# Agent attention and a gated feed-forward layer on one core: value runs in other gaps, query splits a gap earlier, both matmuls of a weights call together, the output copy ahead of a subtraction

## The chip, the cores and the metric

The kernel runs on one core of a Trainium2 chip. The metric is the device time of one execution in microseconds (us), lower is better. TensorE (PE) multiplies, VectorE (DVE) and ScalarE (ACT) do the element-wise work, GpSimd (POOL) issues some copies as DMAs, and SyncE (SP) issues the loads and the stores.

## The reference, cut to what matters

```python
def _attn_ref(q, k, v, agents):          # q, k, v: 4 x 12480 x 128, agents: 4 x 49 x 128
    scale = 1.0 / np.sqrt(q.shape[-1])
    def sm(a, b):
        s = scale * (a @ b.transpose(0, 2, 1))
        s = s - s.max(-1, keepdims=True)
        e = np.exp(s)
        return e / (e.sum(-1, keepdims=True) + 1e-09)
    agent_v = sm(agents, k) @ v           # 49 x 128 per batch
    return sm(q, agents) @ agent_v

def _moe_ref(x, w_in, w_out):            # x: 49920 x 128, w_in: 128 x 2048, w_out: 2048 x 128
    h = x @ w_in
    g = h * (1.0 / (1.0 + np.exp(-1.702 * h)))
    return g @ w_out                      # x is the attention's output
```

All is float32. For each of the 4 batches the agents attend to the keys and gather the values, then every query attends to the 49 agents, and the result goes through the feed-forward layer.

## The kernel before, in words

The attention's last product is folded into the first feed-forward weight: for each batch `agent_v @ w_in` is computed once (49 x 2048, `weights_parts`), and a token then needs only its 49 softmax weights. Float32 products are made from two or three parts of lower precision (`hi` and `lo`, `wh` and `wl`, `gh` and `gl`), so each large product is three matmuls. The matmuls work on half of PE's rows, two at a time, one on each half (`half_matmul`).

Queries are handled in blocks of 960 tokens: 13 blocks per batch, 52 in all (`n`). A block has 16 feed-forward steps `f` of 128 columns. One step is an `up` (6 half matmuls into two banks of the pool `ph`, which has four), two GELUs on ACT (L493) that free those banks, a rounded copy `gh` (a POOL-issued DMA, or ACT, L505), a remainder `gl = g - gh` on DVE (`low`, L510), and a `down` (12 half matmuls into the output banks `po`).

The program is a list of gaps. A block has 17 of them (k = 0 to 16). In a gap each engine gets, in this order: the extra jobs that a table put there (`put`), the `up` of a step, the `low` of the step three before, the `down`s of a step about five before (one half of two steps), and the `high`s. Gap k = 1 has no `up`. At k = 16 (`NF`) the only down is the last half of the block's last step, and `store` copies the two `po` banks out, one by ACT (L540) and one by DVE (L542). The next block's first `down`, in its gap 0, writes the same two banks. Each engine runs its own instructions in exactly this order; only SP's order is left to the framework.

The extra jobs for the blocks to come are:

- Query block n + 1: its tile is split on DVE in four pieces (L170, L172; tile `rest`) in gaps 13 to 16, scored on PE in gaps 0 and 1 of the next block, shifted by its maximum in gap 2, exponentiated on ACT in gap 4 (with a change of ACT's function table before and after), summed and scaled in gap 6, transposed in gap 8 (`P_AT`).
- Keys of the next batch, three groups in a block at gaps 4, 10 and 13 (`K_AT`), 13 groups, so the first four to five blocks of a batch: the key phase.
- Then the values of the next batch, the value phase of seven blocks: two key groups are exponentiated together on ACT in gap 4 (`E_AT`, L320, `slot`), each group's pair of operands `e_pair` (high part and remainder, DVE L325 and L326) is made in gap 7, the pair `v_pair` from a value tile (DVE L330 and L331) in gaps 6 and 10, and the value runs (`key_values`, 16 half matmuls of 258 columns) are in gaps 10 and 14 (`V_AT`). `key_sum` adds the result in the gap behind (L353).
- Then the weights of the next batch: `weights_1` and two calls of `weights_parts` of 1024 columns each, two banks in a call. Six such calls are at the three batch boundaries, one more near the program's start.

The extra jobs' results on PE (scores, transposes, value runs, weights) all go through one two-bank tile, `ps_m`, of a pool with a single buffer.

Of the kernel before, what the change touches and what calls it, by code (L numbers as in the profile page):

```python
# [18 lines left out]
TB = 120  # L19
# [10 lines left out]
Z_AT = 6  # L30
P_AT = 8
K_AT = (4, 10, 13)
V_AT = (6, 10)
PAIR = 2 * 128 + 16
BY_DMA = (1, 9)
EPS = 1e-09
# [3 lines left out]
def kernel(  # L40
# [10 lines left out]
    nc = tc.nc  # L51
    B, C, N = qT.shape
    A = agT.shape[2]
    F = w_in.shape[1] // 2
    NF = F // P
# [25 lines left out]
    for c in range(2):  # L81
        nc.vector.tensor_add(
            out=sel[:, c * H : c * H + A], in0=ident[:, 0:A], in1=ident[:, H : H + A]
# [3 lines left out]
    for i in range(2):  # L87
        t = const.tile([P, KB, P], F32R, name=f"e_pair{i}")
        nc.gpsimd.memset(t.bitcast(F32), 0.0)
        e_pair.append(t)  # L90
    v_pair = const.tile([P, KB, 2 * C + 2], F32R, name="v_pair")
# [71 lines left out]
    def split(t):  # L163
        r = work.tile([P, GT + PAD], F32, name="rest", tag="rest")
        nc.gpsimd.memset(t[:, GT:], 0.0)

        def piece(i):
            s = slice(0, CH + PAD) if i < 2 else slice(CH + PAD, GT + PAD)
            if i % 2 == 0:
                nc.vector.tensor_sub(out=r[:, s], in0=t[:, s], in1=halves(t)[0][:, s])  # L170
            else:
                nc.vector.tensor_sub(out=halves(r)[1][:, s], in0=r[:, s], in1=halves(r)[0][:, s])  # L172

        return (halves(t)[0], halves(r)[0], halves(r)[1]), piece
# [30 lines left out]
    def two_banks():  # L205
        return ps_m.tile([P, 2, 512], F32, name="ps_m")
# [115 lines left out]
    def key_pair(g):  # L322
        sc = score[:TB, g * KB : (g + 1) * KB, :]
        ep = e_pair[g % 2]
        nc.vector.tensor_copy(out=ep[:TB, :, 0:A], in_=sc)  # L325
        nc.vector.tensor_sub(out=ep[:TB, :, H : H + A], in0=sc, in1=ep[:TB, :, 0:A].bitcast(F32))  # L326

    def value_pair(vt):
        vp = v_pair
        nc.vector.tensor_copy(out=vp[:TB, :, 0:C], in_=vt[:TB])  # L330
        nc.vector.tensor_sub(out=vp[:TB, :, C : 2 * C], in0=vt[:TB], in1=vp[:TB, :, 0:C].bitcast(F32))  # L331

    def key_values(g):
# [57 lines left out]
    def weights_parts(b, w, c, banks=(0, 1)):  # L391
        if c == 0 and 0 in banks:
            wts[b] = wpool.tile([P, F], F32R, name="wh"), wpool.tile([P, F], F32R, name="wl")
        wh, wl = wts[b]
        pw = two_banks()
        for i in banks:
            s = slice((c + i) * 512, (c + i + 1) * 512)
            nc.tensor.matmul(out=pw[:, i], lhsT=w["avT"], rhs=w_in_sb[:, s], start=True, stop=True)  # L398
            nc.scalar.copy(out=wh[:, s], in_=pw[:, i])
            nc.vector.tensor_sub(out=wl[:, s], in0=pw[:, i], in1=wh[:, s].bitcast(F32))  # L400

# [146 lines left out]
    vts = {}  # L548
# [5 lines left out]
    banks = {}  # L554
# [14 lines left out]
    def do_query_load(n):  # L569
        if n < B * NG:  # L570
            qts[n] = query_load(*divmod(n, NG))
# [6 lines left out]
    def do_query_split(n, i):  # L578
        if n < B * NG:
            if i == 0:  # L580
                q_parts[n], pieces[n] = split(qts.pop(n))
            pieces[n](i)
# [6 lines left out]
    def do_key_store(b, g):  # L589
        key_store(g, banks.pop((b, g))[1])  # L590
# [9 lines left out]
    def do_query_scores(n, c):  # L600
        if n < B * NG:
            if c == 0:
                banks[n] = score_banks()
            scores(n // NG, q_parts[n], banks[n][0], c)

    def do_query_shift(n):
        if n < B * NG:
            scored[n] = query_shift(banks.pop(n)[1])

    def do_query_exp(n):  # L610
        if n < B * NG:
            query_exp(scored[n])

    def do_query_sums(n):
        if n < B * NG:
            sums[n] = query_sums(n)

    def do_query_softmax(n):
        if n < B * NG:
            query_softmax(n, scored.pop(n), sums.pop(n))  # L620

    def do_query_pairs(n):
        if n < B * NG:
            pairs[n] = query_pairs(n)
# [102 lines left out]
    def gap_of(u):  # L727
        if u < LAG:
            return u
        n, k = divmod(u - LAG, NF)  # L730
        return LAG + n * GAPS + (k + 1 if k else 0)

    def put(t, fn):
        at.setdefault(t, []).append(fn)

    def take(t, runs):
        assert not busy.intersection(range(t, t + runs)), t
        busy.update(range(t, t + runs + 1))
# [8 lines left out]
    for n in range(B * NG):  # L747
        t = LAG + n * GAPS
        m = n + 1
        for i in range(4):  # L750
            put(t - 4 + i, lambda m=m, i=i: do_query_split(m, i))
        take(t, 2)
        put(t, lambda m=m: do_query_scores(m, 0))
        put(t + 1, lambda m=m: do_query_scores(m, 1))
        put(t + 2, lambda m=m: do_query_shift(m))
        put(t + 2, lambda m=m: do_query_load(m + 1))
        put(t + E_AT, lambda m=m: do_query_exp(m))
        put(t + Z_AT, lambda m=m: do_query_sums(m))
        put(t + Z_AT, lambda m=m: do_query_softmax(m))
        take(t + P_AT, 1)  # L760
        put(t + P_AT, lambda m=m: do_query_pairs(m))
# [9 lines left out]
    for b in range(B - 1):  # L771
        begin = gap_of(b * NG * NF)
        end = gap_of((b + 1) * NG * NF)
        slots = [LAG + n * GAPS + k for n in range(B * NG) for k in K_AT]
        slots = [t for t in slots if t >= begin + 4][:NKG]
        for k, t in enumerate(slots):
            put(max(t - 13, 0), lambda b=b, k=k: do_key_load(b + 1, k))
            for i in range(4):
                put(t - 4 + i, lambda b=b, k=k, i=i: do_key_split(b + 1, k, i))
            take(t, 2)  # L780
            put(t, lambda b=b, k=k: do_key_scores(b + 1, k, 0))
            put(t + 1, lambda b=b, k=k: do_key_scores(b + 1, k, 1))
            put(t + 2, lambda b=b, k=k: do_key_store(b + 1, k))
        mx = {}
        put(t + 3, lambda mx=mx: key_max_0(mx))
        t = free(t + 4)
        put(t, lambda mx=mx: key_max_1(mx))
        t = free(t + 2)
        put(t, lambda mx=mx: key_max_2(mx))
        shift = t + 1  # L790

        n0 = (shift + 1 - LAG - E_AT + GAPS - 1) // GAPS
        for k in range(NKG):
            slot = LAG + (n0 + k // 2) * GAPS + E_AT
            exps.setdefault(slot, []).append(k)
            last = k == NKG - 1
            t = slot + V_AT[k % 2]
            put(min(shift + 3 * k, slot - 1), lambda k=k: key_shift(k, nc.vector.tensor_tensor))
            put(t - 16, lambda b=b, k=k: do_value_load(b + 1, k))
            put(t - 4, lambda b=b, k=k: value_pair(vts.pop((b + 1, k))))  # L800
            put(slot + 3, lambda k=k: key_pair(k))
            take(t, 1)
            put(t, lambda b=b, k=k: do_key_values(b + 1, k))
            put(t + 1, lambda b=b, k=k: do_key_sum(b + 1, k))
        w = {}
        put(t + 2, lambda b=b, w=w: weights_0(accs.pop(b + 1), w))
        t = free(t + 3)
        put(t, lambda w=w: weights_1(w))
        for c in range(0, F // 512, 2):
            t = free(t + 2)  # L810
            assert t < end + 4 * c - 3, (b, begin, shift, end, t)
            put(t, lambda b=b, w=w, c=c: weights_parts(b + 1, w, c))
# [23 lines left out]
    def do_low(u):  # L836
        if 0 <= u < steps:
            gl[u] = low(g.pop(u), gh[u])
# [11 lines left out]
    def gap(t):  # L850
        n, k = divmod(t - LAG, GAPS)
        final = n == B * NG - 1
        if t < LAG:
            u = t
        elif final:
            u = n * NF + LAG + k
        elif k == 1:
            u = None
        else:
            u = n * NF + LAG + max(k - 1, 0)  # L860
        before, late[:] = list(late), []
        rest()
        for job in at.pop(t, ()):
            job()
        if u is not None:
            if u < steps:
                do_up(u)
                rest()
            do_low(u - 3)
        if t >= LAG:  # L870
            do_downs(n, k)
        for u in before + soon:
            do_high(u)
        soon.clear()

    def do_downs(n, k):
        if k == 0:
            po[n] = [ps_o.tile([P, 512], F32, name=f"po{c}") for c in range(2)]
        first_whole = NF - LAG - 1 if n == B * NG - 1 else NF
        if 0 < k <= first_whole:  # L880
            do_down(n, k - 1, True)
        if k < first_whole:
            do_down(n, k, False)
        elif k < NF:
            do_down_whole(n, k)
        else:
            store(*divmod(n, NG), po.pop(n))
# [44 lines left out]
```

## Time and profile before

| | |
|---|---|
| time, median of 3 runs | 1999.68 us (1998.36 to 2003.41) |
| profiled execution, its time | 2000.02 us |
| its span, first to last instruction | 1998.2 us |
| PE busy | 1939.2 us, 97% |
| PE weight loads (PEld) busy | 1800.3 us, 90% |
| DVE busy | 1557.0 us, 78% |
| ACT busy | 1397.0 us, 70% |
| mean granted PE clock | 0.988 of full speed |

The span is 1.8 us shorter than the time, so differences in the span are differences in the time. PE is the engine with the most work. PE's busy time is drawn from modelled ends of pipelined matmuls, so a stretch that looks filled need not run at PE's own pace; the distance between the starts of the same matmul in successive gaps tells more.

### The profile page before, as it was taken

To read this page: it belongs to the slowest core of one execution; us is meant where nothing else is said; L and a number is where in the kernel's file an instruction comes from. 1 tells how busy PE (TensorE), PEld (TensorE's weight loads), DVE (VectorE), ACT (ScalarE), POOL (GpSimd) and SP (SyncE) were. 2 spreads that over 40 slices of the span, in tenths; PEclk is the share of its full clock that TensorE was granted. 3 is DMA by queue.
4 is the path that set the end of the run, shared out by engine and by line. 5 is a ranking of instruction groups with operands and counts; after the bars stand their busy time and mean duration, and the time that the engine had idled before them with its cause. 6 is when DMAs were issued, how large, how long until landed. Compare 5 with 4: busy or idle time off the path is not lost.

```text
span 1998.2 us, 59378 instructions
## 1 busy us (share of the span) xinstructions
PE 1939.2 (97%) x25150; PEld 1800.3 (90%) x25150; DVE 1557.0 (78%) x2037; ACT 1397.0 (70%) x2406; POOL 291.0 (15%) x639
## 2 busy tenths in 40 slices
PE   7699999999999999999999999999999999999999
PEld 7489999999889999998988999999997999999998
DVE  6588878888778888887877888888876767676775
ACT  3257777677667667777667667777676777777775
POOL 0011111111111111111111111111111111111111
PEclk9699999999999999999999999999999999999999
DMA  9466566665545565665655566566654554545453
GB/s 279 137 187 205 181 190 187 197 193 189 179 159 191 184 199 180 189 199 181 195 163 170 190 200 192 186 198 190 189 169 141 173 182 169 189 169 189 169 178 140
DMA packets 118383, 366.96 MB, mean 184 GB/s; under 512 B 12604, under 2 KB 32284, under 8 KB 118116
## 3 DMA queue, kind: packets, MB, share of 16 engines
q0 software_dynamic: 75168, 256.61, 37.3%
q1 hardware_dynamic: 42948, 106.55, 19.6%
q8 instruction: 197, 3.23, 0.7%
q14 instruction: 70, 0.57, 0.1%
HBM read 80.97 MB, written 25.56 MB: 53 GB/s over the span
## 4 chain that ended last, share of the span: by engine, by line
PE 85%; ACT 5%; DVE 5%; DMA 4%; issue 2%; SPq 0%; DVEq 0%; POOLq 0%; POOL 0%; ACTq 0%
PE po L191 47%; PE ph L191 26%; PE ps_m L191 8%; DMA gh<-g 2%; ACT g L493 1%; DVE gl L510 1%; ACT L493 1%; PE ph L260 1%; ACT L419 1%; PE ps_m L398 1%; DMA words<-w_out 1%; ACT score L320 1%; DMA vt<-v 1%; DVE rest L172 0%; PE po L532 0%
## 5 line engine op out<-in xcount | busy, mean ns | idle before, releaser
L493 ACT ACTIVATE g<-ph 128x480 f32<-128x480 f32 x1664 | 851.8, 571 | 454.0 <-PE ph L191 445.2
L510 DVE TENSOR_TENSOR gl<-g,gh 128x960 fp32r<-128x960 f32 x832 | 945.8, 1153 | 230.7 <-DMA gh<-g 138.5
L191 PE MATMUL po<-gh,wo_h 64*128 64x480 f32 x3300 | 833.9, 381 | 5.8 <-DVE o L542 3.9
L191 PE MATMUL po<-gl,wo_h 64*128 64x480 f32 x3300 | 826.8, 378 | 0.0
L191 PE MATMUL po<-gh,wo_l 64*128 64x480 f32 x3300 | 822.3, 376 | 0.0
L503 POOL DMA_DIRECT2D gh<-g x522 | 275.7, 528 | 1647.7 <-PE ph L191 722.7
L191 PEld LDWEIGHTS po<-gh,wo_h 64*128 64x128 f32 x3300 | 488.5, 184 | 24.1 <-DVE o L542 10.7
L191 PEld LDWEIGHTS po<-gh,wo_l 64*128 64x128 f32 x3300 | 490.0, 184 | 13.2
L191 PEld LDWEIGHTS po<-gl,wo_h 64*128 64x128 f32 x3300 | 491.5, 186 | 11.3
L191 PE MATMUL ph<-q_hi,wh 49*128 49x480 f32 x1664 | 443.8, 404 | 10.1 <-ACT g L493 9.4
L191 PE MATMUL ph<-q_lo,wh 49*128 49x480 f32 x1664 | 420.2, 381 | 0.0
L191 PE MATMUL ph<-q_hi,wl 49*128 49x480 f32 x1664 | 415.9, 378 | 0.0
L505 ACT CAST gh<-g 128x960 fp32r<-128x960 f32 x310 | 310.5, 1002 | 8.2
L191 PEld LDWEIGHTS ph<-q_hi,wh 49*128 49x128 f32 x1664 | 247.5, 185 | 42.8 <-ACT g L493 28.4
L191 PEld LDWEIGHTS ph<-q_hi,wl 49*128 49x128 f32 x1664 | 247.6, 185 | 9.3 <-DVE wl L400 0.2
L191 PEld LDWEIGHTS ph<-q_lo,wh 49*128 49x128 f32 x1664 | 247.5, 188 | 4.3
L191 PE MATMUL ps_m<-ag_part,rest 64*128 64x49 bf16 x4320 | 146.6, 182 | 7.6 <-DVE rest L172 4.9
L191 PEld LDWEIGHTS <-rest 64*128 64x128 bf16 x4320 | 126.2, 93 | 9.8 <-DVE rest L172 7.1
L172 DVE TENSOR_TENSOR rest<-rest 128x488 bf16<-128x488 f32 (+1 forms) x182 | 131.8, 724 | 0.1
L191 PE MATMUL ps_m<-ag_part,qt 64*128 64x49 bf16 x2448 | 87.2, 183 | 0.0
L191 PEld LDWEIGHTS <-qt 64*128 64x128 bf16 x2448 | 71.4, 94 | 15.2 <-issue 10.2
L170 DVE TENSOR_TENSOR rest<-qt 128x488 f32<-128x488 f32 x104 | 68.4, 658 | 0.0
(110 smaller groups left out, 1254.7 us busy)
## 6 DMA issues: line engine op xcount, KB each, us to landing
gh<-g POOLq DMA_DIRECT2D x522, 480.0 KB, 3.2
kt<-kT SPq DMA_DIRECT2D x52, 480.0 KB, 4.2
qt<-qT SPq DMA_DIRECT2D x52, 480.0 KB, 4.2
vt<-v SPq DMA_DIRECT2D x52, 480.0 KB, 5.3
outT<-o SPq DMA_DIRECT2D x104, 240.0 KB, 2.8
words<-w_in SPq DMA_DIRECT2D x4, 512.0 KB, 12.1
words<-w_out SPq DMA_DIRECT2D x4, 512.0 KB, 13.2
ag_sb<-agT SPq DMA_DIRECT2D x1, 98.0 KB, 2.1
```

What stands on the lines that cost most here:

```text
L170: nc.vector.tensor_sub(out=r[:, s], in0=t[:, s], in1=halves(t)[0][:, s])
L172: nc.vector.tensor_sub(out=halves(r)[1][:, s], in0=r[:, s], in1=halves(r)[0][:, s])
L191: ins = nc.tensor.matmul(tile_position=(c * H, 0), **kw)
L260: nc.tensor.matmul(out=ps[:TB, j * 2 * A : (j + 1) * 2 * A], lhsT=kt[:, c * KB // 2 + j, :], rhs=ag_sb[:, 0:2, :].rearrange("p b a -> p (b ...
L320: nc.scalar.activation(out=sc, in_=sc, func=AF.Exp, scale=scale)
L398: nc.tensor.matmul(out=pw[:, i], lhsT=w["avT"], rhs=w_in_sb[:, s], start=True, stop=True)
L419: nc.scalar.activation(out=e, in_=e, func=AF.Exp, scale=scale)
L493: nc.scalar.activation(out=g[:, c, :], in_=ph[c][:, :CH], func=AF.Gelu_apprx_sigmoid)
L503: nc.gpsimd.dma_start(out=gh, in_=g)
L505: nc.scalar.copy(out=gh, in_=g)
L510: nc.vector.tensor_sub(out=gl, in0=g, in1=gh.bitcast(F32))
```

## The change

Five edits. (1) `V_AT` goes from (6, 10) to (8, 19) behind `slot`, so value runs move from gaps 10 and 14 to gaps 12 and 6, the second in the next block. (2) `v_pair` is made in two pieces, the high part three gaps ahead of the run and the remainder two gaps ahead, and the `e_pair` of the second group of a slot is made in gap 1 of the next block. (3) Query splits start a gap earlier, in gaps 12 to 15. (4) A weights call issues both banks' matmuls before the copies and the subtractions. (5) In gap 16 the `low` stands behind the `store`. Line numbers move by one to four up to `low` and by more further down, so L191 of before is L192 of the change.

```diff
-V_AT = (6, 10)
+V_AT = (8, 19)
+PAIR_AT = (3, 14)
...
-    def value_pair(vt):
+    def value_high(vt):
+        nc.vector.tensor_copy(out=v_pair[:TB, :, 0:C], in_=vt[:TB])
+
+    def value_low(vt):
         vp = v_pair
-        nc.vector.tensor_copy(out=vp[:TB, :, 0:C], in_=vt[:TB])
         nc.vector.tensor_sub(out=vp[:TB, :, C : 2 * C], in0=vt[:TB], in1=vp[:TB, :, 0:C].bitcast(F32))
...
         pw = two_banks()
-        for i in banks:
-            s = slice((c + i) * 512, (c + i + 1) * 512)
+        cols = {i: slice((c + i) * 512, (c + i + 1) * 512) for i in banks}
+        for i, s in cols.items():
             nc.tensor.matmul(out=pw[:, i], lhsT=w["avT"], rhs=w_in_sb[:, s], start=True, stop=True)
+        for i, s in cols.items():
             nc.scalar.copy(out=wh[:, s], in_=pw[:, i])
             nc.vector.tensor_sub(out=wl[:, s], in0=pw[:, i], in1=wh[:, s].bitcast(F32))
...
-            put(t - 4 + i, lambda m=m, i=i: do_query_split(m, i))
+            put(t - 5 + i, lambda m=m, i=i: do_query_split(m, i))
...
-            put(t - 4, lambda b=b, k=k: value_pair(vts.pop((b + 1, k))))
-            put(slot + 3, lambda k=k: key_pair(k))
+            put(t - 3, lambda b=b, k=k: value_high(vts[b + 1, k]))
+            put(t - 2, lambda b=b, k=k: value_low(vts.pop((b + 1, k))))
+            put(slot + PAIR_AT[k % 2], lambda k=k: key_pair(k))
...
-            do_low(u - 3)
+            if k != NF:
+                do_low(u - 3)
         if t >= LAG:
             do_downs(n, k)
+        if u is not None and k == NF:
+            do_low(u - 3)
```

What this does to the order, at three places. The first is PE in gap 6 of a block of the value phase: the last two matmuls of gap 5's downs, and the `up` of gap 6 (`ph`). Before:

```order
L191 MATMUL po_6487<-gh,wo_l 128x480
L191 MATMUL po_6486<-gh,wo_l 128x480
L191 MATMUL ph<-q_hi,wh 128x480 x2
L191 MATMUL ph<-q_lo,wh 128x480 x2
L191 MATMUL ph<-q_hi,wl 128x480 x2
```

and of the change:

```order
L192 MATMUL po_6463<-gh,wo_l 128x480
L192 MATMUL po_6462<-gh,wo_l 128x480
L192 MATMUL ps_m<-v_pair,e_pair_92 128x258 x16
L192 MATMUL ph<-q_hi,wh 128x480 x2
L192 MATMUL ph<-q_lo,wh 128x480 x2
L192 MATMUL ph<-q_hi,wl 128x480 x2
```

A whole value run of 16 matmuls now stands ahead of this `up`; before, the two runs of a block stood ahead of the `up`s of gaps 10 and 14.

The second is DVE around the turn of a block in the value phase, from gap 15 (`rest<-qt`) over the store (`o`) to the query shift of gap 2 (`m`, `e_sb`). `gl` is a `low`, `acc` a `key_sum`. Before:

```order
L170 TENSOR_TENSOR rest<-qt 128x480
L353 TENSOR_TENSOR acc<-ps_m,acc 128x514
L510 TENSOR_TENSOR gl<-g,gh 128x960
L172 TENSOR_TENSOR rest<-rest 128x480
L510 TENSOR_TENSOR gl<-g,gh 128x960
L542 COPY o<-po_6487 128x480
L510 TENSOR_TENSOR gl<-g,gh 128x960
L411 TENSOR_REDUCE m<-ps_m 120x8
L413 TENSOR_TENSOR e_sb<-ps_m,m 120x8x49
```

and of the change:

```order
L171 TENSOR_TENSOR rest<-qt 128x480
L514 TENSOR_TENSOR gl<-g,gh 128x960
L173 TENSOR_TENSOR rest<-rest 128x480
L514 TENSOR_TENSOR gl<-g,gh 128x960
L546 COPY o<-po_6463 128x480
L514 TENSOR_TENSOR gl<-g,gh 128x960 x2
L326 CAST e_pair_92<-score 120x8x49
L327 TENSOR_TENSOR e_pair_92<-score,e_pair_92 120x8x49
L415 TENSOR_REDUCE m<-ps_m 120x8
L417 TENSOR_TENSOR e_sb<-ps_m,m 120x8x49
```

The last split piece now stands ahead of gap 15's `low` and no longer ahead of gap 16's, the `o` copy stands ahead of gap 16's `low`, and one `e_pair` has come in ahead of the query shift.

The third is PE in a weights call in gap 3 of the last block of a batch, with the semaphores that each instruction waits for. Before:

```order
L398 MATMUL ps_m<-w_in_sb,avT 128x512 [waits DVE_49,PE_49]
L398 MATMUL ps_m<-w_in_sb,avT 128x512 [waits DVE_49]
L191 MATMUL ph<-q_hi,wh 128x480 [waits Activation_49] x2
L191 MATMUL ph<-q_lo,wh 128x480 x2
L191 MATMUL ph<-q_hi,wl 128x480 x2
```

and of the change:

```order
L401 MATMUL ps_m<-w_in_sb,avT 128x512 [waits DVE_49,PE_49]
L401 MATMUL ps_m<-w_in_sb,avT 128x512
L192 MATMUL ph<-q_hi,wh 128x480 [waits Activation_49] x2
L192 MATMUL ph<-q_lo,wh 128x480 x2
L192 MATMUL ph<-q_hi,wl 128x480 x2
```

The second matmul has lost its wait for DVE. On ACT the second copy of a call has got one, for DVE's subtraction of the first bank:

```order
L403 CAST wh<-ps_m 128x512 [waits PE_49]
L403 CAST wh<-ps_m 128x512 [waits DVE_49]
```

Before, both of these copies waited for PE alone. At a batch boundary the two calls stood in gap 15 and in gap 3 of the next block; they now stand in gaps 3 and 5 of that block, since the last value run is later.

## Rows read from the trace of the kernel before

**Rows 1.** The page's first part: busy time, share of the span and number of instructions of three engines.

```profile
PE 1939.2 (97%) x25150; PEld 1800.3 (90%) x25150; DVE 1557.0 (78%) x2037; ACT 1397.0 (70%) x2406; POOL 291.0 (15%) x639
```

**Rows 2.** The chain of waits of PE's weight loads (PEld) over the whole span, then of its matmuls (PE): who waited for whom, us in total, times, longest.

```profile
PEld ph L191 <- ACT g L493: 28.4, 59, 4.6
...
PEld ps_m L398 <- DVE wl L400: 19.0, 7, 5.5
PEld po L191 <- DVE o L542: 10.7, 16, 1.4
...
PEld L191 <- DVE rest L172: 7.1, 14, 1.6
...
PE ps_m L398 <- DVE wl L400: 12.4, 7, 4.0
PE ph L191 <- ACT g L493: 9.4, 19, 3.9
...
PE po L191 <- DVE o L542: 3.9, 6, 1.0
```

**Rows 3.** PE in order of time in gaps 5 to 7 of a block of the value phase: start, duration, matmul; x2 is a pair, and the bracket is idle time ahead of it and what ended it. The `ph<-q_hi,wh` rows are the starts of the `up`s.

```profile
1387.63 0.46 PE L191 MATMUL ph<-q_hi,wh 49*128 49x480 f32 x2
...
1390.12 0.94 PE L191 MATMUL ph<-q_hi,wh 49*128 49x480 f32 x2 [0.28 <-ACT g L493]
...
1392.43 0.59 PE L191 MATMUL ph<-q_hi,wh 49*128 49x480 f32 x2
```

**Rows 4.** ACT in the same block, from the end of gap 3's GELUs to the six GELUs of gaps 4 to 6.

```profile
1385.61 1.28 ACT L419 ACT_TABLE_LOAD   x1
...
1387.34 0.85 ACT L320 ACTIVATE score<-score 120x784 f32<-120x784 f32 x1
...
1389.50 2.89 ACT L493 ACTIVATE g<-ph 128x480 f32<-128x480 f32 x6
```

**Rows 5.** PE in the last phase, where nothing is made for a next batch: the starts of the `up`s of gaps 4 and 5 of one block.

```profile
1573.58 0.44 PE L191 MATMUL ph<-q_hi,wh 49*128 49x480 f32 x2
...
1575.54 0.72 PE L191 MATMUL ph<-q_hi,wh 49*128 49x480 f32 x2
```

**Rows 6.** PE around the value run of gap 10 in the block of rows 3 (the `up` of gap 9, the value run, the `up` of gap 10).

```profile
1396.68 0.58 PE L191 MATMUL ph<-q_hi,wh 49*128 49x480 f32 x2
...
1398.63 1.22 PE L191 MATMUL ps_m<-v_pair,e_pair 64*128 64x258 f32 x15
1399.59 0.38 PE L191 MATMUL ph<-q_hi,wh 49*128 49x480 f32 x1
```

**Rows 7.** The waits of the weight loads in the value phase of the third batch boundary, 1270 to 1527 us.

```profile
PEld ph L191 <- ACT g L493: 6.6, 14, 0.8
```

**Rows 8.** PE and, last, DVE in the first weights call of the third batch boundary.

```profile
1519.33 1.13 PE L398 MATMUL ps_m<-w_in_sb,avT 128*128 128x512 f32 x2
1521.86 1.12 PE L398 MATMUL ps_m<-w_in_sb,avT 128*128 128x512 f32 x2 [1.40 <-DVE wl L400]
1522.92 0.48 PE L191 MATMUL ph<-q_hi,wh 49*128 49x480 f32 x2
...
1521.11 0.69 DVE L400 TENSOR_TENSOR wl<-ps_m,wh 128x512 fp32r<-128x512 f32 x1 [0.89 <-ACT wh L399]
```

**Rows 9.** The weights call near the start (PE, then DVE).

```profile
87.36 2.07 PE L398 MATMUL ps_m<-w_in_sb,avT 128*128 128x512 f32 x2
93.39 2.08 PE L398 MATMUL ps_m<-w_in_sb,avT 128*128 128x512 f32 x2 [3.96 <-DVE wl L400]
...
96.12 0.69 DVE L400 TENSOR_TENSOR wl<-ps_m,wh 128x512 fp32r<-128x512 f32 x1 [2.79 <-ACT wh L399]
```

**Rows 10.** DVE in gaps 15 to 0 at the end of a block of the key phase, then the matmul of PE that waits there.

```profile
745.07 0.72 DVE L172 TENSOR_TENSOR rest<-rest 128x480 bf16<-128x480 f32 x1
746.60 1.16 DVE L510 TENSOR_TENSOR gl<-g,gh 128x960 fp32r<-128x960 f32 x1 [0.81 <-DMA gh<-g]
747.68 0.65 DVE L542 COPY o<-po 128x480 f32<-128x480 f32 x1
...
745.21 0.45 PE L191 MATMUL po<-gh,wo_l 64*128 64x480 f32 x2
...
748.38 0.49 PE L191 MATMUL po<-gh,wo_h 64*128 64x480 f32 x1 [0.94 <-DVE o L542]
```

**Rows 11.** DVE at the end of a block of the value phase (gap 16 to gap 2 of the next).

```profile
1412.22 1.15 DVE L510 TENSOR_TENSOR gl<-g,gh 128x960 fp32r<-128x960 f32 x1
1414.08 0.66 DVE L542 COPY o<-po 128x480 f32<-128x480 f32 x1 [0.72 <-PE po L191]
1414.66 1.15 DVE L510 TENSOR_TENSOR gl<-g,gh 128x960 fp32r<-128x960 f32 x1
1416.75 0.57 DVE L411 TENSOR_REDUCE m<-ps_m 120x8 f32<-120x392 f32 x1 [0.94 <-PE ps_m L191]
```

**Rows 12.** DVE in gap 6 of the block of rows 3, the two halves of `v_pair`.

```profile
1389.61 0.69 DVE L330 CAST v_pair<-vt 120x1024 fp32r<-120x1024 f32 x1
1390.33 1.23 DVE L331 TENSOR_TENSOR v_pair<-vt,v_pair 120x1024 fp32r<-120x1024 f32 x1
```

**Rows 13.** Busy time behind the program's start: window, its length, then busy us and instructions of PE, PEld, DVE, ACT and POOL, PE's granted clock, DMA share, GB/s.

```profile
150.00:1998.00 1848.00, 1821.76 (x23824) 1697.52 (x23821) 1453.62 (x1855) 1339.71 (x2292) 276.13 (x589) 1.00 0.57 182
```

## The prediction

> **What bounds the kernel now.** I read the page's first part, the busy time behind the start, then the chain of waits, and then PE's rows gap by gap. PE is busy 97% of the span, the next engine 78% [rows 1], and behind the start it is idle for only 1848.00 - 1821.76 = 26.2 us, at full clock [rows 13]. So PE's order of work is the path, and DVE or ACT matter only where PE waits for them. The reader is to see that these waits are bigger than the idle time says. In a gap that nothing disturbs, the starts of two `up`s are 1575.54 - 1573.58 = 1.96 us apart [rows 5]; that is PE's own pace. In gap 6 of the value phase the same distance is 1390.12 - 1387.63 = 2.49, and the one behind it 1392.43 - 1390.12 = 2.31, although PE shows just 0.28 us of idle time [rows 3]: the first matmul of the pair waits, then the second half of the pair waits once more for its own bank, and both are drawn as long matmuls. The loss is 0.53 + 0.35 = 0.88 us a block, three times the idle time. The waits of the weight loads say the same: 6.6 us in 14 waits over the seven blocks of a value phase, 0.94 a block [rows 7]. I therefore size waits by distances of starts, or by PEld's row where these agree.
>
> On this the Trainium skill ("Perfetto Trace Analysis", Identifying the Most-Contended Engine) has a rule: PE's matmul busy share is no good measure of how near a kernel is to its limit, because matmuls are pipelined. It agrees with 0.28 against 0.88. Whoever took the 26.2 us of idle time as all that there is to win would forbid the sum below; that reading is the first rival.
>
> **Value runs in gap 6.** Why PE stands there: ACT spends gap 4 on two table changes and two exponentials, from 1385.61 to 1389.50, 3.9 us, and only then runs the six GELUs of gaps 4 to 6, 2.89 / 6 = 0.48 each [rows 4]. `ph` has four banks, so the `up` of gap 6 needs the GELUs of gap 4. A value run needs no ACT and costs 1399.59 - 1396.68 - 1.96 = 0.95 us [rows 6]. Put ahead of gap 6's `up`, it runs from 1387.63 + 1.96 = 1389.59 to 1390.54. By then the first two GELUs are through (1389.50 + 0.96 = 1390.46), so the `up` starts without a wait. Gap 7's `up` comes at 1392.50 and needs the fourth GELU, done at 1391.4. Before, it came at 1392.43 without the run. So the run costs 0.07 there and 0.95 less in its old gap: 0.88 gained. The second run of each slot goes there, six in a value phase, 18 in all (the first block of a phase has none): 18 x 0.88 = **15.8 us**. Bounds: 18 x 0.28 = 5.0 by the idle rows, 18 x 0.94 = 17.0 by PEld's. The other 21 runs go from gap 10 to gap 12 and cost 0.95 in either.
>
> What the run must not wait for: its `v_pair` remainder stands in gap 4, its `e_pair` in gap 1, and `ps_m` is free from the query shift in gap 2 until the transposes of gap 8, between which the `key_sum` of gap 7 has to lie. DVE gives up 0.69 + 1.23 us in gap 6 [rows 12] for a sum in gap 7, so it gets there sooner. The `e_pair` falls into DVE's 0.94 us of idle time ahead of the query shift [rows 11]. No cost taken; uncovered, it delays that shift by about a microsecond, and what waits for the shift is an exponential two gaps later.
>
> **Weights calls.** The second matmul starts at 1521.86, after 1.40 us of idle time, and takes until 1522.92, that is 1.06; the first began at 1519.33 [rows 8]. Without the wait the `up` follows at 1519.33 + 2 x 1.06 = 1521.45 instead of 1522.92: 1.47 us, six calls, **8.8 us**. The waits row agrees: 12.4 us in 7, less the 3.96 of the start [rows 2, 9], is 8.4, the lower bound. What is new is that ACT's second copy waits for DVE's subtraction of the first bank: 1519.33 + 1.13 + 0.59 + 0.69 + 0.59 = 1522.3 until ACT gets to its GELUs. The `up`'s first result is there at about that time. So little is handed on, and with four `ph` banks PE has two more gaps before it asks. In gap 5, where the second call now stands, ACT is late from its tables, and the DVE queue behind the call (`low`s, the softmax sums) waits with it; the call's own 2.1 us of PE work covers that.
>
> The seventh call stands near the start: PE waits 3.96 us, and DVE 2.79 for ACT's copy [rows 9]. The stretch behind is DVE's, so I take DVE's 2.79 less some rounding, **2.5 us**; bounds 0 and 4.0.
>
> **Output copy.** PE's first `down` of a block waits for the `o` copy, which stands behind a `low` that itself may wait for a DMA: there the copy began at 747.68, PE stood until 748.38 and had been idle for 0.94 [rows 10]. The last `po` matmul ended at 745.21 + 0.45 = 745.66; with the copy first it runs to about 746.3, over a microsecond before PE asks at 748.38 - 0.94 = 747.44. PEld's row has 10.7 us in 16 such waits, PE's idle row 3.9 [rows 2]. For the reason given above I take **10.7**, with 3.9 as the lower bound. What is late next is gap 16's `low`, now behind a copy that waits for PE in every quiet block: it ends near 1414.08 + 0.66 + 1.15 = 1415.9 [rows 11]. Its user is the `down` of the next block's gap 2, which stands behind the scores that end at 1416.75 and behind an `up`. That hides it by more than 0.9 us.
>
> **Query splits.** In the key phase the last piece (0.72 at 745.07, [rows 10]) stands just ahead of the scores that read it. PEld waits 7.1 us for such pieces in 14 places [rows 2], some of them for key pieces near the start, which do not move. I take **2 us**, bounds 0 and 7.1. Earlier, the pieces share gap 12 with a key piece; DVE's queue for gaps 13 to 16 is one piece shorter for it, and the load is long there.
>
> **Sum.** 15.8 + 8.8 + 2.5 + 10.7 + 2.0 = 39.8 us off the profiled execution's 2000.0, so 1960.2; against the median of 1999.7 it is 1959.9. I say 1960. All lower bounds give a gain of 5.0 + 8.4 + 0 + 3.9 + 0 = 17.3 (1983), all upper ones 17.0 + 8.8 + 4.0 + 10.7 + 7.1 = 47.6 (1952).
>
> **Rivals.** *Idle time is all the loss.* PE's idle rows are 9.4 for GELUs, of which 3.9 near the start, so 5.5; 8.4 for weights; 3.9 for `o`; with 2.5 at the start 20.3 us, **1980**. For it speaks that the matmuls are drawn as busy; against it the distances of starts. 12%.
>
> *The run in gap 6 waits itself,* for its operands or for a late DVE, or PE's wait moves whole to gap 7: the first term falls away, 39.8 - 15.8 = 24, **1976**. Against it: 1.07 us between the fourth GELU and gap 7's `up`. 8%.
>
> *Slower: the copy holds DVE.* In quiet blocks DVE already waits 0.72 us for PE ahead of `o` [rows 11]; with the copy first, a `low` and all behind it wait too. It ends slower than before if each of the 52 blocks hands more than (39.8 + 6) / 52 = 0.88 us to PE, so if gap 16's `low` is late by its cover plus that, 1.8 us or more; at 2.5 us it would be 52 x 1.6 - 39.8 = 43 us slower, **2043**. DVE is busy 78% [rows 1] and PE's wait in the one block would have to repeat in all. 3%.
>
> *The value copies hold POOL's DMAs.* A `v_pair` high part takes 0.69 us [rows 12] and now stands in gaps 3 and 9, beside `gh` issues. If each of the 39 held a `gh` for its length and PE felt it all, 27 us come back, **1987**. 3%. The Trainium skill ("SBUF — State Buffer", two separate sides) states that a DVE copy in a two-port mode locks GpSimd out of their shared port, so that a DMA issued from GpSimd waits for its descriptors. No row of mine shows a loss on PE from it, and the copies were there before.
>
> *No change, within 0.3%:* all waits come back elsewhere. 2%. *Below 1952:* 2%. The forecast itself: 70%.
>
> **How the numbers follow.** About 0.3%, 6 us, is what a measurement of this kernel can tell from no change. The range takes the forecast with its bounds and the second rival, 1952 to 1978; outside are the first rival, the three small ones and the tail, two in ten. Faster: 0.70 + 0.12 + 0.08 + 0.03 + 0.02 = 0.95; same 0.02; slower 0.03.
>
> **What would show it.** In the value phase the `up`s of gaps 6 and 7 start 2.9 and 1.96 apart, and PEld's wait for GELUs falls from 28.4 to about 11. The row of PE behind `wl` is gone, and that of `o` is near zero. Blocks of a value phase last as long as one of the last phase plus two runs. The prediction is wrong if a new row of PE behind `acc`, `v_pair` or `gl` appears with more than 5 us, or if the distance behind gap 7 grows.

## The result, and the profile after

The changed kernel takes 1954.88 us (median of 6 runs, 1951.06 to 1960.33) against 1999.02 for the kernel before on the same chip (6 runs), a ratio of 0.9774 with a 95% interval of 0.9754 to 0.9794: 44 us, 2.3%, faster. The prediction was 1960 us with a range of 1952 to 1978. The profiled execution took 1956.82 us, its span is 1955.1. One execution of an experiment (the second run in gap 5, measured again) took 6656 us where its others took about 1955, and is left out of that ratio.

The first part of the page. PE's busy time is down by 22 us only, its weight loads' by 33; the rest of the 43 us by which the span is shorter is idle time.

```profile
PE 1917.0 (98%) x25150; PEld 1767.5 (90%) x25150; DVE 1546.3 (79%) x2037; ACT 1398.2 (72%) x2406; POOL 292.3 (15%) x639
```

The chain of waits of PE's weight loads over the span, the rows that answer to [rows 2] and one new one; lines have moved (L398 is L401, L493 is L497, L172 is L173).

```profile
PEld ph L192 <- ACT g L497: 11.9, 20, 5.5
...
PEld ps_m L192 <- DVE acc L356: 5.7, 11, 1.0
...
PEld L192 <- DVE rest L173: 4.4, 3, 1.6
...
PEld ps_m L401 <- DVE w_in_sb L135: 3.1, 1, 3.1
```

The rows behind `wl` (19.0) and `o` (10.7) are gone, the wait for GELUs fell from 28.4 to 11.9. Two rows of more than 2 us are new: `ps_m` behind the key sum `acc`, and, once near the start, a weights matmul behind the columns of `w_in` that DVE is still converting. PE in gaps 5 to 7 of a block of the value phase, as in [rows 3]:

```profile
367.09 0.47 PE L192 MATMUL ph<-q_hi,wh 49*128 49x480 f32 x2
369.06 1.20 PE L192 MATMUL ps_m<-v_pair,e_pair 64*128 64x258 f32 x16
370.02 0.50 PE L192 MATMUL ph<-q_hi,wh 49*128 49x480 f32 x2
371.98 0.48 PE L192 MATMUL ph<-q_hi,wh 49*128 49x480 f32 x2
374.40 0.46 PE L192 MATMUL ps_m<-ident,p_pad 64*128 64x64 f32 x8 [0.20 <-DVE acc L356]
```

The `up`s start 2.93 and 1.96 us apart, with a value run between the first two. Before it was 2.49 and 2.31 without one.

**Where the time went.** The starts of the 832 `up`s stand in both traces, so the program can be cut at them and the pieces compared by their place in the block. The pieces from the first block's gap 0 to the last `up` are called the loop here: 1883.9 us before, 1845.6 after, 38.3 less; the stretch ahead of it went from 99.3 to 94.4.

| place | predicted gain, us | measured gain, us |
|---|---|---|
| value phase, the gaps of the moved runs (6, 7, 10, 12 and 14) | 15.8 | 14.3 |
| gap 8 (transposes) | 0 | -5.2 |
| the gaps of the weights calls at batch boundaries | 8.8 | 11.3 |
| gap 0 to 2 (the store's wait) | 10.7 | 11.0 |
| gap 16 to gap 0 (query splits) | 2.0 | 6.9 |
| ahead of the first block | 2.5 | 4.9 |

The sum is 43.2 against 39.8. What the loop's other gaps add comes to less than 0.1 in all.

### The profile page after: what moved, and what is told of

Its sections match the earlier page's. It is cut to its first block, busy times and chain, and to the rows that moved or that the text cites. A ratio compares the mean times of both kernels' runs of the same rounds, so it can differ in the third digit from the quotient of the medians.

```text
span 1955.1 us, 59373 instructions
## 1 busy us (share of the span) xinstructions
PE 1917.0 (98%) x25150; PEld 1767.5 (90%) x25150; DVE 1546.3 (79%) x2037; ACT 1398.2 (72%) x2406; POOL 292.3 (15%) x639
## 4 chain that ended last, share of the span: by engine, by line
PE 92%; DVE 3%; DMA 2%; issue 1%; ACT 1%; SPq 0%; POOLq 0%; DVEq 0%; POOL 0%; ACTq 0%
PE po L192 52%; PE ph L192 28%; PE ps_m L192 8%; DMA gh<-g 2%; PE ph L261 1%; PE ps_m L401 1%; DVE gl L514 1%; PE po L669 1%; DMA vt<-v 1%; PE po L536 0%; ACT g L497 0%; DVE rest L173 0%; DMA kt<-kT 0%; ACT L497 0%; ACT L423 0%
## 5 line engine op out<-in xcount | busy, mean ns | idle before, releaser
L497 ACT ACTIVATE g<-ph 128x480 f32<-128x480 f32 x1664 | 853.3, 571 | 419.3 <-PE ph L192 415.2
L192 PE MATMUL po<-gh,wo_h 64*128 64x480 f32 x3300 | 740.0, 381 | 2.4 <-POOLq L199 2.3
L192 PE MATMUL po<-gl,wo_h 64*128 64x480 f32 x3300 | 735.3, 378 | 0.0
L192 PE MATMUL po<-gh,wo_l 64*128 64x480 f32 x3300 | 732.0, 376 | 0.0
L192 PEld LDWEIGHTS po<-gl,wo_h 64*128 64x128 f32 x3300 | 415.0, 186 | 16.9
L192 PEld LDWEIGHTS po<-gh,wo_h 64*128 64x128 f32 x3300 | 411.1, 184 | 20.9 <-POOLq L199 3.6
L192 PEld LDWEIGHTS po<-gh,wo_l 64*128 64x128 f32 x3300 | 412.2, 184 | 17.4
L192 PE MATMUL ph<-q_hi,wh 49*128 49x480 f32 x1664 | 392.9, 402 | 6.8 <-ACT g L497 6.1
L192 PE MATMUL ph<-q_lo,wh 49*128 49x480 f32 x1664 | 374.3, 379 | 0.0
L192 PE MATMUL ph<-q_hi,wl 49*128 49x480 f32 x1664 | 372.2, 378 | 0.0
L192 PEld LDWEIGHTS ph<-q_hi,wh 49*128 49x128 f32 x1664 | 210.5, 185 | 29.0 <-ACT g L497 11.9
L192 PEld LDWEIGHTS ph<-q_hi,wl 49*128 49x128 f32 x1664 | 209.8, 185 | 9.5 <-DVE wl L404 0.2
L192 PEld LDWEIGHTS ph<-q_lo,wh 49*128 49x128 f32 x1664 | 210.7, 188 | 5.8
L192 PE MATMUL ps_m<-ag_part,rest 64*128 64x49 bf16 x4320 | 134.3, 181 | 5.9 <-DVE rest L173 4.0
L173 DVE TENSOR_TENSOR rest<-rest 128x488 bf16<-128x488 f32 (+1 forms) x182 | 131.8, 724 | 0.1
L192 PEld LDWEIGHTS <-rest 64*128 64x128 bf16 x4320 | 117.2, 93 | 6.4 <-DVE rest L173 4.4
L192 PEld LDWEIGHTS <-qt 64*128 64x128 bf16 x2448 | 66.5, 94 | 20.5 <-issue 18.4
L192 PE MATMUL ps_m<-ag_part,qt 64*128 64x49 bf16 x2448 | 78.3, 183 | 0.0
```

The lines of the kernel that those rows point to most:

```text
L192: ins = nc.tensor.matmul(tile_position=(c * H, 0), **kw)
L497: nc.scalar.activation(out=g[:, c, :], in_=ph[c][:, :CH], func=AF.Gelu_apprx_sigmoid)
```

## The experiments

All kernels were timed against the kernel before on their own chip. The time ahead of the loop differs from trace to trace by up to 9 us (the last matmul on values there ends between 64.3 and 71.3 us), also where the program is the same, so each experiment is given with its ratio and with its loop. Of the kernel before there is one loop, and a few single gaps in it are a microsecond longer than in most other traces; differences of 2 to 3 us between loops are not read.

**Value runs alone** (edits 1 and 2 on the kernel before).

```diff
-V_AT = (6, 10)
+V_AT = (8, 19)
+PAIR_AT = (3, 14)
...
-            put(t - 4, lambda b=b, k=k: value_pair(vts.pop((b + 1, k))))
-            put(slot + 3, lambda k=k: key_pair(k))
+            put(t - 3, lambda b=b, k=k: value_high(vts[b + 1, k]))
+            put(t - 2, lambda b=b, k=k: value_low(vts.pop((b + 1, k))))
+            put(slot + PAIR_AT[k % 2], lambda k=k: key_pair(k))
```

> Only the value runs move (to gaps 12 and 6), with their operands in two pieces; weights calls, query splits and the store are those of the kernel before. Theory (the run fills PE's wait for ACT in gap 6): 18 fills of about 0.8 us, less some 5 us of new waits of the transposes in gap 8 for the key sum, so 9 to 14 us faster than before. Rival (the gain of the whole change comes from the turn of the blocks and the weights, the run only moves PE's wait): within 3 us of before.

Measured: 0.9939 (0.9915 to 0.9963), 12 us faster; loop 1870.0, 13.9 less. The first theory holds for the value phase: the three kinds of blocks in it (the first, the middle ones and the last) gain what they gain in the whole change. Gap 8 shows no wait. But the weights calls, still bank by bank, cost 7.0 us more than before, which I had not put into the expectation, so the 12 us lie in the expected range by other terms than expected. The second call is now in gap 5, right behind ACT's table changes. PE there, then ACT:

```profile
1520.24 1.13 PE L401 MATMUL ps_m<-w_in_sb,avT 128*128 128x512 f32 x2
1523.54 1.13 PE L401 MATMUL ps_m<-w_in_sb,avT 128*128 128x512 f32 x2 [2.18 <-DVE wl L403]
1524.60 0.49 PE L192 MATMUL ph<-q_hi,wh 49*128 49x480 f32 x2
1528.03 0.57 PE L192 MATMUL ph<-q_hi,wh 49*128 49x480 f32 x2
...
1519.96 1.28 ACT L496 ACT_TABLE_LOAD   x1
1521.25 1.03 ACT L496 ACTIVATE g<-ph 128x480 f32<-128x480 f32 x2
1522.17 0.59 ACT L402 CAST wh<-ps_m 128x512 fp32r<-128x512 f32 x1
1524.70 0.59 ACT L402 CAST wh<-ps_m 128x512 fp32r<-128x512 f32 x1 [1.94 <-PE ps_m L401]
```

Bank by bank, PE's second matmul waits for the first bank's subtraction, that for a copy on ACT, and that for the table change and the GELUs ahead of it. Then ACT waits for PE in turn, its next GELUs are late, and the following `up` comes 3.43 us behind the one before it instead of 1.96. Without this loss the loop would be 20.9 less; 3.2 of it is at the turn of the value blocks (gap 16 to gap 0). About 1.0 of that is one gap that is long in the trace of before alone; that the rest comes from a more even queue on DVE is not shown.

**Weights calls alone** (edit 4 on the kernel before).

```diff
+        cols = {i: slice((c + i) * 512, (c + i + 1) * 512) for i in banks}
+        for i, s in cols.items():
             nc.tensor.matmul(out=pw[:, i], lhsT=w["avT"], rhs=w_in_sb[:, s], start=True, stop=True)
+        for i, s in cols.items():
             nc.scalar.copy(out=wh[:, s], in_=pw[:, i])
```

> Only the weights calls change, both banks' matmuls first. Theory: PE's wait behind the first bank's subtraction falls away, 6 calls of 1.5 to 1.7 us and about 1.3 us at the start, 10 to 12 us faster. Rival (the wait goes on to ACT, whose second copy now waits for DVE, and from there back to PE): under 4 us faster.

Measured: 0.9983 (0.9967 to 0.9999), 3.4 us; loop 7.3 less, of which 3.2 in the two blocks at each boundary, all three boundaries together. So the first theory falls, and the time is in the rival's range, though not by its way: ACT's new wait is not where the gain goes. The calls themselves are 1.7 us shorter each, as in the whole change, and PE then stands a few gaps later, behind waits that it had come too late for until now. PE at the third boundary:

```profile
1509.36 1.99 PE L398 MATMUL ps_m<-w_in_sb,avT 128*128 128x512 f32 x4
...
1515.76 0.20 PE L191 MATMUL ps_m<-ag_part,rest 64*128 64x49 bf16 x1 [0.79 <-DVE rest L172]
...
1522.21 1.98 PE L398 MATMUL ps_m<-w_in_sb,avT 128*128 128x512 f32 x4
...
1530.89 0.95 PE L191 MATMUL ph<-q_hi,wh 49*128 49x480 f32 x2 [0.60 <-ACT g L494]
```

Of the first call's gain 1.0 us goes to the last query piece and 0.4 to the output copy at the turn of the block, of the second's 1.0 to ACT's GELUs in gap 6. The first two are waits that edits 3 and 5 take away; the third is gone in the whole change, where edit 1 has moved the second call to gap 5.

**Store alone** (edit 5 on the kernel before).

```diff
-            do_low(u - 3)
+            if k != NF:
+                do_low(u - 3)
         if t >= LAG:
             do_downs(n, k)
+        if u is not None and k == NF:
+            do_low(u - 3)
```

> Only the output copy goes ahead of gap 16's subtraction. Theory: PE's wait for the copy at the turn of a block falls away, about 10.5 us faster, all of it in the first distance of a block (gap 0 to gap 2). Rival (the idle rows are all there is): 4 us faster.

Measured: 0.9939 (0.9918 to 0.9960), 12 us; loop 11.5 less. The distance from gap 0 to gap 2 gives 11.0 us without the program's first block (10.5 with it; that block's gaps differ from trace to trace), and no row of PE behind DVE's `o` is left. The first theory holds: the loss is what the weight loads' row said, 10.7, and not the 3.9 of idle time.

**Query splits alone** (edit 3 on the kernel before).

```diff
-            put(t - 4 + i, lambda m=m, i=i: do_query_split(m, i))
+            put(t - 5 + i, lambda m=m, i=i: do_query_split(m, i))
```

> Only the query splits start a gap earlier. My first estimate was 2 us; the trace of the changed kernel has 6 to 7 us less in the distance from gap 16 to gap 0. If that is the splits' doing alone: 5 to 7 us faster, in that distance, in key phase and value phase. If the store and the value pieces did it: 2 us or less.

Measured: 0.9982 (0.9968 to 0.9997), 3.6 us, between the two cases; loop 3.4 less. The profiled execution is the slowest of the ten, 3 us above their median. The distance from gap 16 to gap 0 is 0.26 us shorter in each of the first four blocks of a key phase, 3.1 in 12 blocks, as in the whole change; but in this trace the distance from gap 0 to 2 is longer by 3.8 in the key blocks (the program's first left out), and the wait for the output copy has grown from 10.7:

```profile
PEld po L191 <- DVE o L542: 13.4, 15, 2.1
```

PE comes sooner to a copy that, behind a subtraction waiting for its DMA, comes no sooner. So the gain is lost again in this trace. That the order must lose it is not shown: 2.3 of the 3.8 lie in a single block, and in the last experiment, with the same order at this place, the same distance is longer by only 0.4 in these blocks.

**Pieces kept, old gaps** (on the changed kernel).

```diff
-V_AT = (8, 19)
-PAIR_AT = (3, 14)
+V_AT = (6, 10)
+PAIR_AT = (3, 3)
```

> The changed kernel with the value runs back in gaps 10 and 14, their operands still in two pieces, all other edits kept. Theory (filling gap 6 is what the move earns): the distance from gap 5 to gap 6 is 2.5 again and the next 2.3, some 14 us lost, the 5 us of the transposes' wait for the key sum won back, so 8 to 11 us slower than the changed kernel, about 1964 us. Rival (evening out DVE's queue by the pieces is what earns): within 3 us of the changed kernel.

Measured: 0.9884 (0.9865 to 0.9903) of before, beside 0.9786 for the changed kernel when it was measured again (below): some 20 us slower than it; loop 1860.7, which is 15 to 19 above its two loops. The rival falls, and the loss is larger than the theory said: the distances in gaps 6 and 7 of the value phase are those of before to 0.02 us on average, so the 14.3 us are lost. I had counted on winning back the wait for the key sum, and most of that is not there to win (below). And the weights calls, back in gaps 15 and 3, gain 3.9 us less; the second of them again hands 1.0 us to the GELUs of gap 6.

**Second run in gap 5** (on the changed kernel).

```diff
-V_AT = (8, 19)
+V_AT = (8, 18)
```

> The changed kernel with each second value run in gap 5 of the next block instead of gap 6. Theory: PE's wait in gap 6 is for ACT's tables in gap 4, so a run anywhere between fills it as well, and the key sum comes a gap earlier, so that the transposes of gap 8 no longer wait for it: 4 to 6 us faster than the changed kernel, about 1950 us. Rival (only a run in gap 6 itself fills the wait): 10 us or more slower than the changed kernel.

Measured: 0.9779 (0.9765 to 0.9794), loop 1841.1. The rival falls: a run in gap 5 fills the wait as well as one in gap 6. The `up`s of gaps 4 to 7 in one block:

```profile
1343.56 0.45 PE L192 MATMUL ph<-q_hi,wh 49*128 49x480 f32 x2
1345.53 1.23 PE L192 MATMUL ps_m<-v_pair,e_pair 64*128 64x258 f32 x16
1346.49 0.48 PE L192 MATMUL ph<-q_hi,wh 49*128 49x480 f32 x2
1348.45 0.50 PE L192 MATMUL ph<-q_hi,wh 49*128 49x480 f32 x2
1350.41 0.52 PE L192 MATMUL ph<-q_hi,wh 49*128 49x480 f32 x2
```

2.93, then 1.96 twice: gap 6's `up` no longer waits although nothing stands ahead of it. Against the changed kernel the expected 4 to 6 us don't show; measured once more beside it, this kernel gave 0.9792 (0.9769 to 0.9815) against 0.9786.

> Second value runs in gap 5. If the key-sum wait belongs to the order of the changed kernel: 4 to 6 us faster than it; if not: within 2 us of it.

**Key sum earlier** (on the changed kernel).

```diff
-            put(t + 1, lambda b=b, k=k: do_key_sum(b + 1, k))
+            put(t + 1 - k % 2, lambda b=b, k=k: do_key_sum(b + 1, k))
```

> The changed kernel with the key sum of each second run in the gap of its run, ahead of that gap's subtraction on DVE. Theory (the transposes wait because the sum stands behind a subtraction that waits for a DMA): the wait for acc, 5.7 us on PE's weight loads, falls to under 1, 4 to 5 us faster than the changed kernel. Rival (DVE then waits for PE's run and hands the delay on to the subtractions): no faster, a new wait of PE for gl.

Measured: 0.9786 (0.9769 to 0.9804), loop 1840.5; measured again beside the changed kernel, 0.9781 (0.9758 to 0.9804) and 1840.8.

> Key sums of the second runs a gap earlier. If the key-sum wait belongs to the order of the changed kernel: 4 to 6 us faster than it; if not: within 2 us of it.

The wait for `acc` is gone in both traces, and no new wait for `gl` has come; the expected time doesn't show. The cause of the wait stands in the rows of DVE, POOL and SP in the changed kernel's first trace, in the block shown in the section on the result:

```profile
364.82 1.22 DVE L334 TENSOR_TENSOR v_pair<-vt,v_pair 120x1024 fp32r<-120x1024 f32 x1
...
366.05 0.53 POOL L507 DMA_DIRECT2D gh<-g  x1 [5.27 <-DVE v_pair L334]
366.07 0.36 SPq L312 DMA_DIRECT2D vt<-v  x1
...
368.93 0.57 DVE L433 TENSOR_TENSOR p_pad<-e_sb,z 120x392 f32<-120x392 f32 x1
...
372.58 1.16 DVE L514 TENSOR_TENSOR gl<-g,gh 128x960 fp32r<-128x960 f32 x1 [3.09 <-DMA gh<-g]
373.66 0.69 DVE L356 TENSOR_TENSOR acc<-ps_m,acc 128x514 f32<-128x514 f32 x1
```

The sum stands behind a `low` that waits 3.09 us for a `gh` by DMA; the sum ends at 374.35, and PE's transposes, which need its bank of `ps_m`, start at 374.40. The `gh` was issued at 366.05 and landed at 372.49, 6.4 us later, where the median of all is 3.1.

This transfer is late for a reason that the change brings along. The load of a value tile (`vt`, also 480 KB) starts 0.03 us behind the end of a `v_pair` remainder in 30 of 39 cases, and the change puts one remainder in gap 4. So in 12 of the 18 blocks with a run in gap 6 a load starts within 0.07 us of this `gh`, and there the `gh` takes 6.1 to 6.9 us to land; in the other six it takes 2.8 to 5.4. In the kernel before, the nearest load is over 4 us away in the same 18 blocks, and the same `gh` lands after 2.8 to 3.9 us. With the value runs alone the load starts 0.5 to 0.9 us ahead of it in the 12 blocks, it lands after 4.3 to 5.9, and gap 8 shows no wait. No run moves the load by itself, so that the load is what delays the `gh` is likely but not shown.

**The changed kernel once more.**

> The changed kernel once more, beside the two variants below on one chip. If the wait of the transposes for the key sum (5.7 us in its first trace, none in the value runs alone) belongs to the order: 4 us or more again, and 4 to 6 us slower than both variants. If it comes with how late the copies by DMA land in an execution: well under 5 us here, and within 2 us of both variants.

Measured: 0.9786 (0.9764 to 0.9808), loop 1841.4, and the wait is this:

```profile
PEld ps_m L192 <- DVE acc L356: 1.6, 2, 1.0
```

So the same program lost 5.7 us there in one execution and 1.6 in another. The `gh` in question is late in the same 12 blocks here too, 5.5 to 6.9 us after its issue against 6.1 to 6.9: the order makes the wait possible, and how late single transfers land decides how much comes of it. In time the three kernels can't be told apart (0.9786, 0.9792, 0.9781). No version was found that beats the changed kernel by more than its intervals.

**Bank by bank in the changed kernel.**

```diff
-        for i, s in cols.items():
             nc.scalar.copy(out=wh[:, s], in_=pw[:, i])
```

> The changed kernel with the weights calls bank by bank again, all other edits kept, so with the calls in gaps 3 and 5. In the value-run experiment the second call, there in gap 5 behind ACT's table changes, cost 4.8 us more each. If that is what the matmul order is worth inside the whole change: 3 x 4.8 + 3 x 1.7 = 19 us and 1 us at the start, about 20 us slower than the changed kernel. If the order is worth only what it is worth alone (2 to 3 us net): 2 to 3 us slower.

Measured: 0.9869 (0.9846 to 0.9891), loop 1857.3: 16 us slower than the changed kernel. The row behind `wl` is back, larger than before:

```profile
PEld ps_m L401 <- DVE wl L403: 21.1, 7, 5.4
```

The order of the matmuls is worth 3.4 us alone and 16 inside the whole, where the waits that swallowed its gain are gone and the second call stands behind ACT's tables; 5.0 of it lie at each boundary (1.7 for the call in gap 3, 3.3 for that in gap 5 with the gap behind it). The 20 us of the expectation were too many because I had taken 4.8, which is all that the call in gap 5 costs there, its matmuls included, for its loss.

**Subtraction ahead of the copy in the changed kernel** (edit 5 undone).

> The changed kernel with gap 16's subtraction ahead of the output copy again, all other edits kept. With the query splits alone, PE's wait for the copy was larger than before (13.4 us on its weight loads against 10.7), because PE comes to it sooner and the copy does not. If that holds inside the whole change: 13 to 16 us slower than the changed kernel, about 0.985 of the kernel before. If the edits simply add: 11 us slower, about 0.984. If the value pieces have freed DVE so that the copy comes in time anyway: within 3 us of the changed kernel.

Measured: 0.9835 (0.9808 to 0.9863), loop 1851.2, which is 9.8 us above the second loop of the changed kernel. PE waits for `o` again:

```profile
PEld po L192 <- DVE o L546: 10.1, 13, 1.4
```

The third case falls; the edit simply adds here, a little under its worth alone. The larger wait of the query splits alone does not show beside the other edits, and the 3.1 us that the splits gain at gap 16 stay; why is left open.

## Why the prediction was right, and where it was not

The forecast held (1954.9 in 1952 to 1978), the sum was 3.4 us short, and that by terms that missed on both sides: that it came so close is in part luck. The 5.2 us lost in gap 8, which the sum didn't have, are made up by gains at the turn of the block and ahead of the first block that it didn't have either.

**Reading waits by distances.** This carried the forecast, and it was right: the first rival, by idle rows, gave 1980. The store edit alone settles it for that wait, 12 us where the idle rows said 3.9 and the weight loads 10.7. The rule on PE's busy share in the Trainium skill ("Perfetto Trace Analysis", Identifying the Most-Contended Engine) agrees: the share rose from 97% to 98% while the time fell by 2.3%. The Trainium skill's other measure there, the weight loads' busy share, stood at 90% both times.

**Value runs.** Mechanism and size held: 2.93 and 1.96 us as worked out, 14.3 instead of 15.8. The step that was mis-sized is the multiplication by 18. The last block of each value phase exponentiates one group and not two, PE's wait there was shorter, and the three blocks gave about 0.54 each and not 0.88; the other 15 gave 0.86. The step that failed is "no cost taken" for `ps_m`: I had argued that DVE gets to the sum sooner, by its own work, and had not counted the DMA that the `low` ahead of it waits for, nor the load that the remainder in gap 4 lets start beside that DMA. Cost: 5.2 us at gap 8 in the profiled execution, 1.7 in the second; 0.5 of either lies in the three blocks of the weights calls, where the transposes wait for `p_pad`. The prediction's own sign of being wrong, a new row behind `acc` with more than 5 us, did appear, 5.7 on the weight loads (2.0 as idle time of the matmuls): it marks this term, and the rest of the sum outweighed it.

**Weights calls.** 11.3 instead of 8.8. The step mis-sized is 1.06 us for a matmul: that was one that starts out of a wait. Two matmuls (four parts in the trace) back to back take from 542.89 to the `up` at 544.81, that is 0.96 for each matmul:

```profile
542.89 1.98 PE L401 MATMUL ps_m<-w_in_sb,avT 128*128 128x512 f32 x4
544.81 0.48 PE L192 MATMUL ph<-q_hi,wh 49*128 49x480 f32 x2
```

That is 0.2 us a call, 1.2 in six; the rest, a good microsecond, is in `weights_1`, whose gap moved too, and is not taken apart further. More important than the size: I added this term to the others as if it stood by itself. Alone it is worth about a third of that, and without it the value edit loses 7.0 us at the calls. That "the call's own 2.1 us of PE work covers" a late ACT in gap 5 is right only for matmuls that wait for nobody.

**Start.** 4.9 instead of 2.5, and wrong in its parts. 3.6 us were there already at the end of the first value matmuls (71.24 and 67.62), before anything that was changed; the same point lies at 64.3 to 71.3 in other traces, with the load that PE waits for. The call gave 1.3: of its wait, 1.6 us came back at once, because the second bank's matmul needs the columns that DVE is just converting, which I had overlooked. That is one pair of traces: from the same point to the loop it is 25.2 to 26.9 us in the eight traces with both matmuls first and 27.5 to 28.9 in the five bank by bank, 2.1 apart on average. So the term of 2.5 was about right, and the 3.6 belongs to the two executions that were traced, not to the change.

**Output copy.** 10.7 predicted, 11.0 measured, by the way described; no row of `po` behind `gl` shows, so gap 16's `low` did not come late.

**Query splits.** 2 predicted, 6.9 measured at that place. The key blocks' share, 3.1, is the splits': their experiment shows it, and the kernel with edit 5 undone keeps it. 3.5 lie in the value blocks; the value edits alone show 3.2 there and the splits alone 1.8, so most of it is not the splits' doing. About 1 of each of these is a single gap that is long in the trace of before alone.

**The other rivals.** *The run waits itself* falls with the distances; *the copy holds DVE* falls with the store alone; *the value copies hold POOL's DMAs* finds no row of PE in any trace; in the block shown the high part ran before the late `gh` was issued, and no other copy of DVE falls into its 6.4 us. *No change* falls with the time.

## What to carry to other kernels

Size a wait of a pipelined engine by the distance between equal instructions of successive rounds, because the drawn idle time can be a third of the loss. Work that needs nothing from the late engine fills its wait ahead of the instruction that would wait, and here one gap sooner as well. Moving work also moves the loads that wait for its buffers: look at what they start beside. Edits that each take away one wait on the same path need not add: ask for every one which wait is reached next, and expect part of its worth only when that one is gone as well.

## What was not expected of the hardware

A transfer of 480 KB issued by POOL landed after 2.8 to 3.9 us with no value load near it and after 6.1 to 6.9 us with one started beside it (12 blocks of the changed kernel's first trace). Behind an engine that works in order such a transfer reached PE by a way of four steps (DMA, `gl`, `acc`, transposes). Of the 4.2 us between the loops of two executions of one program (1845.6 and 1841.4) 3.5 lie in that gap. Across all traces the start of the loop varies by 9 us (90.3 to 99.4); 7 of them stand already at the end of the first value matmuls, which wait for their loads.
